# Row statistics of tile 2 computed once, and two other constants for instruction blocks in the planner, in a retention + SoLU + cosine-gate kernel

## The chip, the cores and the metric

One core of a Trainium2 chip. The time is that of one execution on the device in microseconds, from its start to its end; shown are medians over runs. The profile is one more execution, recorded by the hardware profiler; its own time stands beside its span, which runs from the first to the last recorded instruction.

## The reference

Three stages over 4 x 768 = 3072 tokens of width 512:

```python
# 1: retention, 4 batches x 8 heads, head width 64
state = gamma * state + k[t] (x) v[t]
y[t]  = scale * q[t] @ state
# 2: x is y with the heads side by side, (3072, 512)
h    = x @ w_in                       # 512 -> 1024
e    = exp(h - max(h)); sm = e / (sum(e) + 1e-9)
solu = h * sm
ln   = (solu - mean(solu)) / sqrt(var(solu) + 1e-6) * g_ln
x2   = ln @ w_out                     # 1024 -> 512
# 3
h2   = x2 @ w_in2                     # 512 -> 2048
out  = (h2 * cos(h2)) @ w_out2        # 2048 -> 512
```

max, sum, mean and var run over the 1024 columns of a row.

## The kernel before, in words

**Stage 1** goes in 24 steps of 128 tokens (2 pairs of batches x 12 chunks of 64 tokens). `load_step` (L366 on) brings a step's q, k and v in two transfers into one of four buffers `in` (in the listings `in_162` to `in_165`); `prep` scales keys and queries; `scores` and the step before multiply keys by queries into PSUM tile `sc` (L409), `masks` turns that into `s` on VectorE (L354); `step` computes the output `y` (L427) and the new state `S` (L415). What comes out of a step, split into a high and a low part `xh`, `xl`, is the left operand of stage 2: step n gives *tile* n, 128 tokens. Tiles 2 and 3 keep `xh`, `xl` in a corner of `o1h`, `o1l`.

**Stage 2** multiplies a tile by `w_in` (`mm1`, L633; four blocks k of the 512 inputs, two halves c of the 1024 columns, three products for each k: `w1h,xh`, `w1h,xl`, `w1l,xh`), into PSUM: `hA` (two banks of 512 columns), or, for tiles 0, 2 and 4, `hB` (three banks). Tile 0 has banks 0 and 1 of `hB`, tile 2 has banks 1 and 2: its half 0 shares bank 1 with tile 0's half 1. `norm(n)` then computes the row statistics of tile n from both halves: a maximum over 1024 columns (L651, VectorE), an Exp with its sum (ScalarE, L351, tile `u`), a product with its sum (L362, VectorE), a Square with its sum (ScalarE), a chain of one-column operations on tiles `sm` (`sm_77` to `sm_79`, three in turn), a power on POOL (L660) and the normalisation of `u` on VectorE (L664) or ScalarE. Then `transp` (L678) transposes four tiles at a time into PSUM tiles `tr`, which are opened where `hB` was once tile 4 is through (`open_tr`), and `mm2` (L703) multiplies by `w_out`.

`chunk(c, k, tiles)` issues the products of one k and one half c, the two with `w1h` first and `w1l` behind; `first(n, c)` issues all of one half, and calls `norm(n)` where c is 1:

```python
def first(n, c):
    for k in range(KD):
        mm1(n, c, k)
    if c == 1:
        norm(n)
```

Near the program's start tile 2's half 1 is issued before its half 0, as `first(2, 1)` (L1085), between the last products of tile 0 (`chunk(0, k, (0,))`, which calls `norm(0)`) and the scores of step 3. Half 0 follows later, as `first(2, 0)`, and then `norm(2)` by name. So `norm(2)` stands twice: once ahead of half 0, when bank 1 of `hB` still holds tile 0's columns, and once behind it. The second overwrites everything that the first has written.

**Stage 3** forms the products with `w_in2` and `w_out2` with seven half-size products in place of eight (L879, L960), the cosine between them on ScalarE and VectorE; weights are split on chip during stage 2, written to memory and read back.

**The order of the work** on each engine is the planner's. `Plan.add` records every operation with an engine, a cost and the keys that it reads and writes; `Plan.order` plays them through a model: TensorE takes one of the next 10 in program order (`WINDOW`), the other engines what can start first, among near equals what has the longest way to the end. The list that results is then issued as it stands, and the framework adds semaphores where tiles are shared; it sees `hB` as one tile. An engine posts its count only at instructions that another one waits for.

The model also counts TensorE's instructions (`ni`; a weight load and a matmul are two) in blocks of 256, the first ending after 256 - 63. When a block begins, the next one is taken to arrive `FETCH[1]` us later, or `FETCH[2]` if the time is past `FETCH[0]`; no operation of that block is placed sooner:

```python
fetched[0] += self.count[i]
if fetched[0] // self.BLOCK[1] > was:
    blocks.append(max(t + occ, blocks[-1]) + self.FETCH[1 if t < self.FETCH[0] else 2])
```

These are constants of the planner alone; they reach the chip only through the order.

Of the kernel before, what the change touches and what calls it, by code (L numbers as in the profile page):

```python
# [32 lines left out]
KD = DM // 128  # L33
# [15 lines left out]
class Plan:  # L49
# [17 lines left out]
    LOOK = .1  # L67
    FIRST = (16, 0.97, 0.6)
    BLOCK = (63, 256)
    FETCH = (30.0, 6.3, 4.0)  # L70

    def __init__(self):
        self.ops = []
# [49 lines left out]
    def order(self):  # L123
# [62 lines left out]
        while left:  # L186
# [36 lines left out]
            if e == "PE":  # L223
# [3 lines left out]
                if fetched[0] // self.BLOCK[1] > was:  # L227
                    blocks.append(max(t + occ, blocks[-1]) + self.FETCH[1 if t < self.FETCH[0] else 2])
            else:
# [28 lines left out]
def body(ctx: ExitStack, tc: tile.TileContext, qkv, consts,  # L258
# [126 lines left out]
    def prep(n):  # L385
        i = steps[n][1]
        if i:
            P.add("POOL", 1.2, lambda: nc.gpsimd.tensor_tensor(  # L388
                out=a_p[n % 2].rearrange("p (a b) t -> p a b t", b=2),
                in0=a_q[n % NA].rearrange("p (a b) t -> p a b t", b=2),  # L390
                in1=gat.unsqueeze(2).to_broadcast([128, NHP, 2, C]), op=ALU.mult),
                [("gat",), ("in", n % NA, 1)], [("x32", n % 2)], port=True)
        if has_state(n):
            k = a_kn[n % NA]
            for a in range(NHP):
                f = cs[:, 1, i, a:a + 1]
                act(k[:, a], k[:, a], AF.Copy, [("cs",), ("in", n % NA, 2)], [("ks", n % NA, a)], 0.295,
                    alt=("DVE", 0.2, lambda k=k[:, a], f=f: nc.vector.tensor_scalar(
                        out=k, in0=k, scalar1=f, scalar2=None, op0=ALU.mult), True), scale=f)
# [225 lines left out]
    def mm1(n, c, k, ms=(0, 1, 2)):  # L625
        h, hk = hbank(n, c)
        xh, xl = xhs[xb(n)], xls[xb(n)]
        xhk, xlk = xk[xb(n)]

        def mm():  # L630
            for m in ms:
                a, lo = ((xh, 0), (xl, 0), (xh, 1))[m]
                nc.tensor.matmul(out=h, lhsT=a[:, k], rhs=w1[lo][k][c], start=(k + m == 0), stop=(k == KD - 1 and m == 2))  # L633
        r = [xhk]
        if 0 in ms or 1 in ms:
            r += [("w1h", k, c)]
        if 1 in ms:
            r += [xlk]
        if 2 in ms:
            r += [("w1l", k, c)]  # L640
        P.add("PE", 0.2267 * len(ms), mm, r, [hk], lat=0.2267 * len(ms) + 0.25, ni=2 * len(ms))

    def norm(n):
        b = [hbank(n, c) for c in (0, 1)]
        h = h_of(n)
        hk = [b[0][1], b[1][1]]
        sm = sms[n % 3]
        smk = lambda *c: [("sm", n % 3, x) for x in c]
        u = us[n % UBUF]
        uk = [("u", n % UBUF, c) for c in (0, 1)]  # L650
        P.add("DVE", 1.135, lambda: nc.vector.tensor_reduce(  # L651
            out=sm[:, 0:1], in_=h, axis=AX.XY, op=ALU.max, negate=True), hk, smk(0))
        act(u, h, AF.Exp, hk + smk(0), uk + smk(1), 1.1, 1.35, bias=sm[:, 0:1], accum_out=sm[:, 1:2])
        stt(u, u, 1.0, h, ALU.mult, ALU.mult, hk, uk + smk(2), 1.18, accum_out=sm[:, 2:3])
        ts(sm[:, 3:4], sm[:, 2:3], -1.0 / FF1, None, ALU.mult, None, smk(2), smk(3), 0.07)
        act(junk, u, AF.Square, uk + smk(3), [("junk",)] + smk(4), 1.14, 1.38, bias=sm[:, 3:4], accum_out=sm[:, 4:5])
        ts(sm[:, 5:6], sm[:, 1:2], 1e-9, None, ALU.add, None, smk(1), smk(5), 0.07)
        stt(sm[:, 6:7], sm[:, 5:6], 1e-6, sm[:, 5:6], ALU.mult, ALU.mult, smk(5), smk(6), 0.07, port=True)
        stt(sm[:, 7:8], sm[:, 4:5], 1.0 / FF1, sm[:, 6:7], ALU.mult, ALU.add, smk(4, 6), smk(7), 0.07, port=True)
        P.add("POOL", 0.56, lambda: nc.gpsimd.tensor_tensor(out=sm[:, 8:9], in0=sm[:, 7:8], in1=mhalf, op=ALU.pow),  # L660
              smk(7), smk(8), port=True)
        tt(sm[:, 9:10], sm[:, 3:4], sm[:, 8:9], ALU.mult, smk(3, 8), smk(9), port=True, occ=0.07)
        act(u, u, AF.Identity, smk(8, 9), uk, 1.14,
            alt=("DVE", 0.75, lambda: nc.vector.tensor_scalar(  # L664
                out=u, in0=u, scalar1=sm[:, 8:9], scalar2=sm[:, 9:10], op0=ALU.mult, op1=ALU.add), True),
            scale=sm[:, 8:9], bias=sm[:, 9:10])
# [379 lines left out]
# [6 lines that stand above are left out]
    def chunk(c, k, tiles=(0, 1)):  # L1052
        for ms in ((0, 1), (2,)):
            for n in tiles:
                mm1(n, c, k, ms)
                if c == 0 and k == KD - 1 and 2 in ms:
                    norm(n)
# [24 lines left out]
    P.chained(False)  # L1082
    for k in range(KD):
        chunk(0, k, (0,))
    first(2, 1)  # L1085
    prep(3)
    scores(3)
    for k in range(KD):
# [171 lines left out]
```

## Time and profile before

| | |
|---|---|
| median of 3 runs | 839.0 us (837.82 to 840.07) |
| the profiled execution | 837.1 us, of which 835.3 us span |
| TensorE (PE) busy | 817.4 us, 98% |
| weight loads (PEld) | 717.0 us, 86% |
| VectorE (DVE) busy | 649.0 us, 78% |
| ScalarE (ACT) busy | 506.4 us, 61% |
| POOL busy | 48.6 us, 6% |
| mean granted TensorE clock | 0.999 |

TensorE is busy nearly throughout, so the time is its work and the gaps in it. In rows of the trace a matmul's length contains the part that overlaps the next one: full matmuls of 512 columns start 0.23 us apart, though each is 0.39 us long; VectorE's passes over 512 columns start 0.6 us apart, those over 1024 columns 1.14 us.

### The profile page before, as it was taken

The page shows a single profiled execution, that of the slowest core. Times are in us where ns is not written, and L with a number is a line of the kernel's source. Part 1 is how long each engine was busy: PE and PEld are TensorE (multiplying, and loading weights), DVE is VectorE, ACT ScalarE, POOL GpSimd, SP SyncE. Part 2 cuts the span into 40 slices and gives each one's busy share as a digit, 9 for nine tenths or more (in the row PEclk, how much of TensorE's full clock was granted, in tenths as well). Part 3 has the DMA queues.
Part 4 walks back from the last instruction along what each step waited for, and adds up shares of the span by engine and source line. Part 5 has one row for each costly group of instructions (what it writes and reads, how often), then busy time and mean ns, then how long its engine had stood idle before and what let it go on. Part 6 is the DMA issues. An engine that isn't in the chain of part 4 may idle for free.

```text
span 835.3 us, 18919 instructions
## 1 busy us (share of the span) xinstructions
PE 817.4 (98%) x7312; PEld 717.0 (86%) x7312; DVE 649.0 (78%) x1157; ACT 506.4 (61%) x893; POOL 48.6 (6%) x56
## 2 busy tenths in 40 slices
PE   5899999999999999999999999999999999999997
PEld 4778888888888888888889999888999988889997
DVE  4789988879888677338789993787999648779953
ACT  4688857656666466346785463676746446665452
POOL 2221210111101000000000000000000000000000
PEclk9999999999999999999999999999999999999999
DMA  9893699899976649246665688767667787666563
GB/s 353 326 336 114 194 320 342 270 322 300 323 271 224 219 161 319 86 131 195 192 207 184 198 257 246 233 192 197 201 195 209 198 271 194 196 191 188 181 193 83
DMA packets 93513, 188.19 MB, mean 225 GB/s; under 512 B 9712, under 2 KB 25328, under 8 KB 93424
## 3 DMA queue, kind: packets, MB, share of 16 engines
q1 hardware_dynamic: 92816, 186.41, 70.1%
q8 instruction: 58, 0.95, 0.5%
q10 hardware_dynamic: 608, 0.57, 0.2%
q14 instruction: 31, 0.25, 0.1%
HBM read 145.01 MB, written 41.94 MB: 224 GB/s over the span
## 4 chain that ended last, share of the span: by engine, by line
PE 90%; DMA 4%; DVE 3%; SPq 1%; ACT 1%; issue 1%; ACTq 0%
PE U L879 27%; PE pa L960 15%; PE hA L633 13%; PE y L703 11%; PE U L960 8%; PE pb L960 4%; PE y L427 4%; PE hB L633 2%; PE tr L678 2%; PE tr L703 2%; DMA big<-w_in_dram 1%; DMA in<-qkv_dram 1%; PE sc L409 1%; DVE u L362 1%; DMA y1d<-ys 1%
## 5 line engine op out<-in xcount | busy, mean ns | idle before, releaser
L960 PE MATMUL pa<-wr,gh 128*128 128x256 f32 x768 | 139.8, 283 | 0.0
L902 ACT ACTIVATE gh<-A 128x512 fp32r<-128x512 f32 x144 | 90.7, 630 | 78.6 <-PE pa L960 43.6
L904 DVE TENSOR_TENSOR gl<-A,gh 128x512 fp32r<-128x512 f32 x144 | 98.6, 686 | 29.7 <-ACT gh L902 29.6
L960 PEld LDWEIGHTS pa<-wr,gh 128*128 128x128 f32 x768 | 120.2, 192 | 0.5
L960 PE MATMUL pa<-wr,gl 128*128 128x256 f32 x384 | 108.7, 283 | 0.0
L703 PE MATMUL y<-lt,o1h 128*128 128x512 f32 x304 | 101.9, 399 | 0.0
L960 PEld LDWEIGHTS pa<-wr,gl 128*128 128x128 f32 x384 | 73.7, 192 | 0.0
L960 PE MATMUL U<-wr,gh 128*128 128x256 f32 x384 | 70.3, 283 | 0.0
L703 PEld LDWEIGHTS y<-lt,o1h 128*128 128x128 f32 x304 | 57.1, 188 | 12.2
L633 PE MATMUL hA<-w1h,xh 128*128 128x512 f32 x160 | 64.4, 403 | 0.3 <-DVE u L362 0.2
L633 PE MATMUL hA<-w1l,xh 128*128 128x512 f32 x160 | 62.5, 391 | 0.0
L633 PE MATMUL hA<-w1h,xl 128*128 128x512 f32 x160 | 62.4, 390 | 0.0
L960 PEld LDWEIGHTS U<-wr,gh 128*128 128x128 f32 x384 | 59.9, 192 | 0.0
L703 PE MATMUL y<-lt,o1l 128*128 128x512 f32 x152 | 59.3, 390 | 0.0
L351 ACT ACTIVATE st<-wt 128x512 fp32r<-128x512 f32 (+1 forms) x60 | 35.8, 601 | 33.7 <-DMA wd<-st 17.8
L960 PE MATMUL U<-wr,gl 128*128 128x256 f32 x192 | 54.3, 283 | 0.0
L354 DVE TENSOR_TENSOR st<-wt,st 128x512 fp32r<-128x512 f32 (+1 forms) x60 | 40.5, 678 | 17.0 <-ACT st L351 16.8
L427 PE MATMUL y<-s,in 64*64 64x64 f32 x736 | 45.0, 226 | 1.1 <-DVE s L354 1.1
L427 PEld LDWEIGHTS y<-s,in 64*64 64x64 f32 x736 | 36.4, 138 | 9.2 <-issue 4.6
L427 PE MATMUL y<-x,st 64*64 64x64 f32 x672 | 40.3, 218 | 0.0
L388 POOL TENSOR_TENSOR x<-in,c_all 128x512 f32<-128x512 f32 x22 | 30.5, 1385 | 141.2 <-issue 88.2
L960 PEld LDWEIGHTS U<-wr,gl 128*128 128x128 f32 x192 | 36.9, 192 | 0.0
(180 smaller groups left out, 2082.6 us busy)
## 6 DMA issues: line engine op xcount, KB each, us to landing
wr<-wd SPq DMA_DIRECT2D x168, 256.0 KB, 3.0
wr<-td SPq DMA_DIRECT2D x168, 256.0 KB, 3.0
in<-qkv_dram SPq DMA_DIRECT2D x48, 512.0 KB, 6.2
wd<-st SPq DMA_DIRECT2D x28, 512.0 KB, 4.9
td<-st SPq DMA_DIRECT2D x24, 512.0 KB, 3.5
raw<-w_in_dram SPq DMA_DIRECT2D x16, 511.8 KB, 6.0
raw<-w_out_dram SPq DMA_DIRECT2D x16, 511.8 KB, 5.0
y1d<-ys SPq DMA_DIRECT2D x24, 256.0 KB, 3.7
```

The costliest lines, as they stand in the source:

```text
L351: return P.add("ACT", occ, lambda: nc.scalar.activation(out=out, in_=in_, func=func, **kw), r, w, lat, alt=alt)
L354: return P.add("DVE", occ, lambda: nc.vector.tensor_tensor(out=out, in0=a, in1=b, op=op), r, w, port=port)
L362: return P.add("DVE", occ, lambda: nc.vector.scalar_tensor_tensor(out=out, in0=a, scalar=s, in1=b, op0=op0, op1=op1, **kw), r, w, port=port)
L388: P.add("POOL", 1.2, lambda: nc.gpsimd.tensor_tensor(out=a_p[n % 2].rearrange("p (a b) t -> p a b t", b=2), in0=a_q[n % NA].rearrange("p ( ...
L427: nc.tensor.matmul(out=ybank(n)[0][o, j], lhsT=a[r, j], rhs=b[r, j], start=not part, stop=bool(part) or not later)
L633: nc.tensor.matmul(out=h, lhsT=a[:, k], rhs=w1[lo][k][c], start=(k + m == 0), stop=(k == KD - 1 and m == 2))
L678: nc.tensor.transpose(out=trs[s][:, t * 128:(t + 1) * 128], in_=us[(4 * g + t) % UBUF].rearrange("p c f -> p (c f)")[:, j * 128:(j + 1) * ...
L703: nc.tensor.matmul(out=y1(), lhsT=w[:, j, ds], rhs=lts[j][:, a], start=(j + m == 0), stop=(j == K1 - 1 and m == 2))
L879: nc.tensor.matmul(out=U(), lhsT=p2["wr"][w][:, kk, lo], rhs=p2["x"][m][xl][:, kk], start=(kk + q == 0 and m in (0, 1, 4)), stop=(kk == 1 ...
L902: P.add("ACT", 0.54, lambda: nc.scalar.activation(out=p2["gh"][i], in_=src(), func=AF.Copy), [key], [("gh", i)], after=(*p2["cos_hook"], * ...
L904: P.add("DVE", 0.6, lambda: nc.vector.tensor_tensor(out=p2["gl"][i], in0=src(), in1=p2["gh"][i].bitcast(F32), op=ALU.subtract), [key, ("gh ...
L960: nc.tensor.matmul(out=o, lhsT=p2[x][g][:, t * 128:t * 128 + 128], rhs=v[:, lo], start=(fresh and t % 2 == 0 and i == 0), stop=(s == 7 and ...
```

## The change

Tile 2's half 1 is issued with `chunk(1, k, (2,))` for each k: the same products, without the call of `norm(2)` that stood ahead of half 0. `norm(2)` now stands once, behind half 0. And `FETCH` holds three other numbers: the next block arrives 5.8 us after a block's begin up to 60 us, 4.5 us later on (before: 6.3 us up to 30 us, then 4.0).

```diff
@@ -67,7 +67,7 @@
     LOOK = .1
     FIRST = (16, 0.97, 0.6)
     BLOCK = (63, 256)
-    FETCH = (30.0, 6.3, 4.0)
+    FETCH = (60.0, 5.8, 4.5)
 
     def __init__(self):
         self.ops = []
@@ -1082,7 +1082,8 @@
     P.chained(False)
     for k in range(KD):
         chunk(0, k, (0,))
-    first(2, 1)
+    for k in range(KD):
+        chunk(1, k, (2,))
     prep(3)
     scores(3)
     for k in range(KD):
```

The planner makes another list of it. TensorE's differs in four places: two around the end of tile 2's half 1, one at the first transposes, and one group of four transposes near the end of stage 2. VectorE's, ScalarE's and the transfers' lists are the same up to about 31 us and then differ until the end of stage 2. TensorE, from the last products of tile 0's half 0 (`hB<-..,xh_126`) to tile 1's first (`hA`); `..,o1h` and `..,o1l` are tile 2's half 1, `sc<-in_165` the scores of step 3; the semaphores that an instruction waits for stand in brackets. Before:

```order
L633 MATMUL hB<-w1h_89,xh_126 128x512 [waits Activation_49]
L633 MATMUL hB<-w1h_89,xl_128 128x512
L409 MATMUL sc<-in_165 64x64 [waits DMAHW0_49]
L409 MATMUL sc<-in_165 64x64 x7
L633 MATMUL hB<-w1l_97,xh_126 128x512 [waits DVE_49]
```

and, ten matmuls on, the end of the same stretch as a piece of the difference:

```order
 L633 MATMUL hB<-w1h_90,o1h 128x512
 L633 MATMUL hB<-w1h_90,o1l 128x512
+L633 MATMUL hB<-w1l_99,xh_126 128x512 [waits DVE_49]
 L633 MATMUL hB<-w1l_98,o1h 128x512
-L633 MATMUL hB<-w1l_99,xh_126 128x512 [waits DVE_49]
 L633 MATMUL hB<-w1h_92,o1h 128x512
 L633 MATMUL hB<-w1h_92,o1l 128x512
-L633 MATMUL hB<-w1l_100,o1h 128x512
-L409 MATMUL sc<-in_165 64x64 x8
+L633 MATMUL hB<-w1l_100,o1h 128x512 [waits DVE_49]
+L409 MATMUL sc<-in_165 64x64 [waits DMAHW0_49]
+L409 MATMUL sc<-in_165 64x64 x15
```

The eight scores that stood ahead of `w1l_97` have moved behind tile 2's half 1, to the other eight; tile 0's last product (`w1l_99,xh_126`) stands one place earlier; and the last product of tile 2's half 1 (`w1l_100,o1h`) has got a wait for VectorE.

VectorE at the same place, from the last of the weights' low halves to tile 0's product (`u_104`). Before:

```order
L354 TENSOR_TENSOR w1l_99<-big_123,w1h_91 128x512 [waits Activation_49]
L398 TENSOR_SCALAR in_162<-in_162,c_all 128x128 [waits DMAHW3_49]
L398 TENSOR_SCALAR in_162<-in_162,c_all 128x128
L651 TENSOR_REDUCE sm_77<-hB 128x1 [waits PE_49]
L651 TENSOR_REDUCE sm_79<-hB 128x1
L354 TENSOR_TENSOR s_167<-sc,c_all 128x256 [waits PE_49]
L362 SCALAR_TENSOR_TENSOR u_104,sm_77<-u_104,hB 128x1024 [waits Activation_49]
L362 SCALAR_TENSOR_TENSOR u_106,sm_79<-u_106,hB 128x1024
```

Now:

```order
L354 TENSOR_TENSOR w1l_99<-big_123,w1h_91 128x512 [waits Activation_49]
L398 TENSOR_SCALAR in_162<-in_162,c_all 128x128 [waits DMAHW3_49]
L398 TENSOR_SCALAR in_162<-in_162,c_all 128x128
L651 TENSOR_REDUCE sm_77<-hB 128x1 [waits PE_49]
L398 TENSOR_SCALAR in_163<-in_163,c_all 128x128 [waits DMAHW5_49]
L398 TENSOR_SCALAR in_163<-in_163,c_all 128x128
L354 TENSOR_TENSOR s_167<-sc,c_all 128x256 [waits PE_49]
L354 TENSOR_TENSOR s_167<-sc,c_all 128x256
L398 TENSOR_SCALAR in_163<-in_163,c_all 128x128
L362 SCALAR_TENSOR_TENSOR u_104,sm_77<-u_104,hB 128x1024 [waits Activation_49]
```

Tile 2's early maximum (`sm_79<-hB`) and product (`u_106`) are gone, scalings of keys stand there, and both mask passes `s_167` follow the maximum of tile 0. In the built program the count for which `w1l_100,o1h` waits is the one that this maximum posts, and the maximum's own wait is for a count that TensorE posts at `w1h_92,o1l`, the matmul just ahead of `w1l_100,o1h`.

VectorE some 25 us later, from just behind the maximum of tile 3 (`sm_77<-hA`) and two passes `o1l<-big_116`, `o1l<-big_117`, to the maximum of tile 4 (`sm_78<-hB`); `big` and `o1l` are weights of `w_out` on their way to two halves. Now:

```order
L362 SCALAR_TENSOR_TENSOR big_118<-big_118,top_158 128x512
L362 SCALAR_TENSOR_TENSOR u_107,sm_77<-u_107,hA 128x1024
L358 TENSOR_SCALAR sm_77<-sm_77 128x1 x2
L362 SCALAR_TENSOR_TENSOR sm_77<-sm_77 128x1
L362 SCALAR_TENSOR_TENSOR o1l<-big_118,gcol,o1h 128x512
L362 SCALAR_TENSOR_TENSOR big_119<-big_119,top_159 128x512
L362 SCALAR_TENSOR_TENSOR big_120<-big_120,top_158 128x512
L362 SCALAR_TENSOR_TENSOR sm_77<-sm_77 128x1
L398 TENSOR_SCALAR in_163<-in_163,c_all 128x128
L362 SCALAR_TENSOR_TENSOR o1l<-big_119,gcol,o1h 128x512
L651 TENSOR_REDUCE sm_78<-hB 128x1
```

Between the same two maxima the list before has one pass each of `big` and `o1l`, the normalisation of tile 0 and the product of tile 3; now it has three of `big`, four of `o1l` and the product, and behind the second maximum stand one small operation, a state pass, a mask pass and the product of tile 4 (`u_108<-u_108,hB`) in place of two small ones, the state pass, the normalisation of tile 2, another small one, the mask pass and that product. On TensorE the first eight transposes (`tr`), whose first waits for VectorE, stand behind 12 products of tile 5, and behind 15 before.

## Rows read from the trace of the kernel before

**Rows 1.** The page, busy time (share of the span) and instructions of each engine.

```profile
PE 817.4 (98%) x7312; PEld 717.0 (86%) x7312; DVE 649.0 (78%) x1157; ACT 506.4 (61%) x893; POOL 48.6 (6%) x56
```

**Rows 2.** By stretches, core 0: us, busy us (x instructions) of each engine, clock, DMA share, GB/s.

```profile
40.00:50.00 10.00, 8.44 (x155) 6.87 (x155) 9.61 (x26) 7.54 (x14) 3.25 (x4) 1.00 0.89 330
50.00:60.00 10.00, 8.21 (x156) 6.81 (x155) 7.84 (x17) 7.88 (x19) 3.21 (x3) 1.00 0.96 338
...
sum 835.30, PE 817.45 PEld 717.02 DVE 649.05 ACT 506.38 POOL 48.63; mean PE 35.54 PEld 31.17 DVE 28.22 ACT 22.02 POOL 2.11
```

**Rows 3.** Waits of TensorE, whole span: total us, times, longest us.

```profile
PE sc L409 <- DMA in<-qkv_dram: 5.7, 1, 5.7
PE hA L633 <- issue: 1.8, 1, 1.8
```

**Rows 4.** Timeline of TensorE, 29 to 35 us: start us, length us, instruction.

```profile
29.71 0.68 PE L409 MATMUL sc<-in 64*64 64x64 f32 x16
30.38 0.50 PE L633 MATMUL hB<-w1l,xh 128*128 128x512 f32 x1
...
33.71 0.39 PE L633 MATMUL hB<-w1h,o1l 128*128 128x512 f32 x1
33.94 0.39 PE L633 MATMUL hB<-w1l,o1h 128*128 128x512 f32 x1
34.25 0.68 PE L409 MATMUL sc<-in 64*64 64x64 f32 x16
34.87 0.50 PE L633 MATMUL hA<-w1h,xh 128*128 128x512 f32 x1
```

**Rows 5.** Timeline of VectorE, 29 to 50 us.

```profile
29.65 0.68 DVE L354 TENSOR_TENSOR w1l<-big,w1h 128x512 fp32r<-128x512 f32 x1
...
34.36 2.35 DVE L651 TENSOR_REDUCE sm<-hB 128x1 f32<-128x1024 f32 x2 [2.11 <-PE hB L633]
...
40.29 1.21 DVE L362 SCALAR_TENSOR_TENSOR u<-u,hB 128x1024 f32<-128x1024 f32 x1
...
49.76 0.81 DVE L664 TENSOR_SCALAR u<-u,sm 128x1024 f32<-128x1024 f32 x1
```

**Rows 6.** Timeline of TensorE, 39.6 to 41.9 us, in brackets idle time and its releaser.

```profile
39.68 0.22 PE L409 MATMUL sc<-in 64*64 64x64 f32 x2
41.56 0.50 PE L633 MATMUL hB<-w1h,o1h 128*128 128x512 f32 x1 [1.66 <-DVE u L362]
```

**Rows 7.** The page, DMA queue of instructions: packets, MB, share of 16 engines.

```profile
q8 instruction: 58, 0.95, 0.5%
```

**Rows 8.** The same queue from 41.9 to 42.1 us, and from 53.2 to 53.3 us.

```profile
q8 instruction: 1, 0.02, 27.5%
...
q8 instruction: 1, 0.02, 58.2%
```

**Rows 9.** By stretches of 128 matmuls each; those across an edge are counted on both sides.

```profile
38.30:44.76 6.46, 4.80 (x140) 3.89 (x133) 5.62 (x9) 4.92 (x12) 1.27 (x1) 1.00 0.97 379
...
50.28:55.60 5.32, 3.57 (x134) 3.08 (x135) 4.08 (x8) 5.06 (x14) 2.00 (x2) 1.00 0.96 326
```

**Rows 10.** Timeline of TensorE, 53.3 to 55.9 us.

```profile
55.64 0.39 PE L633 MATMUL hA<-w1h,o1h 128*128 128x512 f32 x1 [1.79 <-issue]
```

**Rows 11.** Timeline of VectorE, 56 to 68 us.

```profile
56.52 1.23 DVE L651 TENSOR_REDUCE sm<-hA 128x1 f32<-128x1024 f32 x1 [1.74 <-PE hA L633]
...
58.78 0.69 DVE L362 SCALAR_TENSOR_TENSOR big<-big,top 128x512 int32<-128x512 int32 x1
...
60.92 0.75 DVE L362 SCALAR_TENSOR_TENSOR o1l<-big,gcol,o1h 128x512 fp32r<-128x512 f32 x1
...
61.96 1.22 DVE L651 TENSOR_REDUCE sm<-hB 128x1 f32<-128x1024 f32 x1 [0.29 <-PE hB L633]
...
66.33 1.21 DVE L362 SCALAR_TENSOR_TENSOR u<-u,hB 128x1024 f32<-128x1024 f32 x1
```

**Rows 12.** Timeline of TensorE, 67 to 68.5 us.

```profile
67.69 1.06 PE L678 MATMUL tr<-ident,u 128*128 128x128 f32 x8
```

## The prediction

> **What bounds the kernel now.** I began with the page's busy times [rows 1]: TensorE works 817.4 of 835.3 us, so only 17.9 us of gaps can be won or lost unless matmuls are added or taken away, and this change does neither. The stretches show where gaps lie [rows 2]: the clock is at full speed (1.00), and 40 to 50 and 50 to 60 us lack 1.56 and 1.79 us of TensorE. The waits of TensorE [rows 3] name two of the long ones: 5.7 us ahead of the first matmul, for the first transfer, which the change does not touch, and 1.8 us before a product into `hA`, put down to "issue", that is to no semaphore. The timelines show the rest: 1.66 us before the product at 41.56, released by VectorE [rows 6], and the 1.79 us of "issue" end at 55.64 [rows 10]. Everything that the change moves lies between 29 us and the end of stage 2, so I go through these gaps in order of time, and ask of each whether it goes, stays, or comes back elsewhere.
>
> **Term 1, the early statistics leave: -1.7 us.** VectorE loses an early maximum (two maxima take 2.35 us together, so some 1.2), a product at 40.29 of 1.21 us and a normalisation at 49.76 of 0.81 us [rows 5]: 3.2 us of work, and ScalarE loses an Exp and a Square beside it. Nearly all lies beside matmuls and is worth nothing by itself. One piece is on TensorE's path. The product at 40.29 reads bank 1 of `hB`, which tile 2's half 0 is about to overwrite; it ends at 41.50, and the first matmul of that half starts at 41.56 [rows 5, 6]. Without it only tile 0's own product has to be done there. That needs tile 0's maximum, one Exp and itself, in a row some 1.2 us each [rows 5], behind a maximum that now starts near 34 us; it is done near 38, while TensorE is busy until 39.9. So the whole gap of 1.66 us goes.
>
> **Term 2, a new wait at the end of tile 2's half 1: +1.5 us.** In the lists of the change the last product of that half, `w1l_100,o1h`, waits for the count that tile 0's maximum posts, and that maximum itself waits for the matmul just ahead. So a maximum of 1024 columns, 1.22 us long when it stands alone [rows 11], now lies between two neighbours on TensorE. Before, the neighbours started 0.23 us apart (33.71 and 33.94) [rows 4], and the maximum started at 34.36, 0.03 us after the last one's end (33.94 + 0.39 = 34.33) [rows 4, 5]. Now: the predecessor's whole 0.39, the maximum's 1.22, some 0.1 for the two signals (an estimate: one is 0.03 as above, the other 0.06, from the product's end at 41.50 to the start at 41.56 [rows 5, 6]), less 0.23, makes 1.47. Queued behind it on TensorE are 16 scores and all of tile 1. Nothing hides it.
>
> **Term 3, eight scores no longer fill a wait: +0.5 us.** `w1l_97` is written by VectorE from 29.65 to 30.33 and read by the matmul at 30.38 [rows 4, 5]. Before, TensorE spent the wait on eight scores (29.71, 0.68 us; the trace counts each row of the list double). Now it stands idle there for about 0.75 us (30.38 - 29.71, and the change of shape that is saved), and the eight cost their time later, 0.62 (34.25 to 34.87) [rows 4], less some 0.1 for one change of shape fewer (ahead of a score block matmuls start 0.31 apart, 33.94 to 34.25, in place of 0.23 [rows 4]).
>
> **Term 4, TensorE runs into its own instructions earlier: +1.3 us.** The queue of instructions moved 58 packets of 16 KB [rows 7], and TensorE issues 14,624 of the program's instructions [rows 1], so a packet is a block of some 252, or about 126 matmuls. When the matmul at 55.64 waits for "issue" [rows 10], a packet of that queue is in flight from 53.2 us [rows 8]: TensorE goes on 2.4 us after its start. That block's predecessor began at 50.28, so the block came 5.36 us after it. The packet at 41.9 us [rows 8], plus the same 2.4, gives 44.3, which is 6.0 us after its predecessor's begin at 38.30; it was wanted at 44.76, so there were 0.4 us to spare [rows 9]. Exactly there term 1 takes 1.7 us out of TensorE's time: the stretch of 6.46 becomes 4.8, and the block, if it still takes 6.0 to 6.1, comes 1.3 late. The upper bound is 1.7 (it took at most 6.46, since no wait showed). The lower one is nothing, if it comes within 4.8; with the 5.36 of the other block it would be 0.6. I take 1.3 because that is this very block, at nearly the same time of the same transfers (DMA share 0.97 [rows 9]). The 1.79 us at 55.64 stay: the order of TensorE's instructions between is the same, and so is what each block holds.
>
> Beside these rows stands a rule. The Trainium skill (Runtime: NRT & Kernel Launch, Instruction fetch mechanics) says that the sequencer fetches the next 16 KiB, 256 instructions, while it executes the current ones, so that crossing such a border is mostly hidden. By that rule term 4 is nothing and the sum below 1.1. The trace here agrees on the size of a block and disagrees on the hiding, with 1.79 us of idle "issue" while a packet is in flight.
>
> **Term 5, the first transposes wait for VectorE: +0.8 us.** They go where `hB` was, so they wait for tile 4's product. Measured from the start of tile 3's maximum (56.52), TensorE reached them 11.17 us later, at 67.69 [rows 11, 12], when that product (66.33, 1.21 us) had just ended, at 67.54. Now they stand three matmuls, 0.7 us, earlier: 10.5. VectorE has more to do between the two maxima: four passes `o1l` and three `big` at their pace of 0.6 to 0.66 us (single rows 0.75 and 0.69 [rows 11]), two passes over 1024 columns at 1.15 and some 0.5 of small operations make 7.3 in place of 61.96 - 56.52 = 5.44. From the second maximum to the product's end it has less: 1.15, two passes of 0.6 and 1.15, 3.5 to 4 in all, in place of 5.6 (61.96 to 67.54). Together 10.9 to 11.4, so a wait of 0.4 to 0.9 and some signalling: I take 0.8. Bounds: nothing, if the passes keep their closest pace, and 2.4, if the second stretch stays at 5.6, for then the product ends at 7.3 + 5.6 = 12.9.
>
> **At no cost.** The other constants make no instruction; they act only through the list. One POOL operation is gone; no gap that I take rests on POOL. The transfers that change places on SP's queue and the scalings of keys now ahead of tile 0's mask passes concern steps read later or halves that are there by then; I allow -0.5 to +1 for them and for the changed list after 70 us.
>
> **The sum:** -1.7 + 1.5 + 0.5 + 1.3 + 0.8 = +2.4 us on a profiled execution of 837.1 us, so 839.5. That execution is 1.9 below the median of 839.0, so against medians I forecast **841.4 us**.
>
> **The rivals.** *Instructions come in time:* term 4 is nothing, the sum +1.1, the time 840.1. For it speaks that a block came in 5.36 us at another place, against it the stall with a packet in flight. *Slower, because the transposes wait:* tile 4's product stays as late behind its maximum as it was, the wait is 2.4 in place of 0.8, the sum +4.0, the time 843.0. It decides as soon as the wait passes 0.9 us, since then the change is slower by more than 0.3% (2.5 us, about what a measurement of this kernel can tell). For it speaks that VectorE's list there also holds waits for ScalarE that were not filled before; against it that a normalisation stands there no longer. *The gain is kept:* the new wait of term 2 does not bite (the count is posted in time by something else) and instructions come in time: -1.7 + 0.5 + 0.8 = -0.4, 838.6. For it speaks only that I read that wait off a list and not off a trace. That the early statistics do not leave is excluded by VectorE's list.
>
> **How the numbers follow.** The forecast has 0.45, its own range 840.0 to 842.8; instructions in time 0.25; the waiting transposes 0.20; the kept gain 0.10. Range: 838.0 to 844.0, from just below the kept gain to the waiting transposes with term 4 at its bound. Faster than 836.5 needs the kept gain and another 2 us that no row shows: 0.05. Slower than 841.5 are the waiting transposes (0.20), just under half of the forecast (0.20) and a little of the second case: 0.42. The rest, 0.53, is no change.
>
> **What would show it.** The gap at 41.56 gone; one of about 1.5 us at 34 us before the last product of tile 2's half 1, and one of 0.75 before `w1l_97`; an "issue" gap near 45 us, and the old one of 1.8 us near 57; a wait for VectorE before the first `tr`. Wrong, if TensorE's idle time between 29 and 70 us falls by more than 1 us, or if the difference arises after 70 us.

## The result: 845.6 us, slower by 0.84%

Four runs of the change have a median of 845.62 us (845.01 to 847.16), beside 838.62 for the kernel before, timed with them; the ratio is 1.0084, with a 95% interval of 1.0065 to 1.0104. The forecast was 841.4, in a range of 838.0 to 844.0: the sign is right, the size is not, and the time lies outside the range. The profiled execution took 847.2 us, of which 845.4 are span; that of the kernel before took 837.1, so the two profiles lie 10 us apart where the medians lie 7.0 apart. The page's busy times, beside [rows 1]:

```profile
PE 822.1 (97%) x7312; PEld 718.5 (85%) x7312; DVE 647.6 (77%) x1165; ACT 500.3 (59%) x872; POOL 52.4 (6%) x55
```

VectorE and ScalarE are busy for less time, as the change promises, but VectorE by 1.4 us only, where term 1 takes 3.2 us from it. In e3_drop below, which takes out the early statistics and moves nothing, the page reads

```profile
PE 818.0 (98%) x7312; PEld 716.7 (86%) x7312; DVE 646.8 (77%) x1148; ACT 504.0 (60%) x889; POOL 49.6 (6%) x55
```

Against it the change has 17 instructions more on VectorE and 17 fewer on ScalarE: passes `in<-in,c_all`, scalings of keys, which the new list gives to VectorE. TensorE, with the same 7312 matmuls, has 4.7 us more of busy time, and 845.4 - 822.1 = 23.3 us of idle time in place of 17.9. Its waits over the whole span, beside [rows 3]:

```profile
PE hA L633 <- issue: 2.8, 1, 2.8
PE tr L678 <- DVE lt L690: 2.6, 3, 1.3
...
PE hB L633 <- DVE sm L651: 1.3, 1, 1.3
...
PE hA L633 <- DVE u L362: 0.9, 2, 0.7
PE S L415 <- issue: 0.8, 2, 0.5
PE tr L678 <- ACT ys L708: 0.5, 1, 0.5
```

The wait for the early product ([rows 6]) is gone; all of these are new or longer than before. In order of time, the timeline of TensorE (start, length, instruction, idle time ahead of it and its releaser):

```profile
31.27 0.50 PE L633 MATMUL hB<-w1l,xh 128*128 128x512 f32 x1 [0.61 <-DVE w1l L354]
...
34.58 0.39 PE L633 MATMUL hB<-w1h,o1l 128*128 128x512 f32 x1
36.28 0.50 PE L633 MATMUL hB<-w1l,o1h 128*128 128x512 f32 x1 [1.32 <-DVE sm L651]
36.71 1.15 PE L409 MATMUL sc<-in 64*64 64x64 f32 x32
...
46.75 0.27 PE L415 MATMUL S<-in 64*64 64x64 f32 x2 [0.47 <-issue]
...
52.80 0.27 PE L415 MATMUL S<-in 64*64 64x64 f32 x1 [0.28 <-issue]
...
59.28 0.50 PE L633 MATMUL hA<-w1h,o1h 128*128 128x512 f32 x1 [2.82 <-issue]
...
60.93 0.63 PE L633 MATMUL hB<-w1h,xh 128*128 128x512 f32 x1
61.35 0.63 PE L633 MATMUL hB<-w1h,xl 128*128 128x512 f32 x1
...
138.13 1.25 PE L678 MATMUL tr<-ident,u 128*128 128x128 f32 x8 [0.90 <-DVE lt L690]
...
148.73 0.50 PE L633 MATMUL hA<-w1h,xh 128*128 128x512 f32 x1 [0.73 <-DVE u L362]
...
340.92 0.66 PE L678 MATMUL tr<-ident,u 128*128 128x128 f32 x4 [0.47 <-ACT ys L708]
...
347.22 0.66 PE L678 MATMUL tr<-ident,u 128*128 128x128 f32 x4 [1.30 <-DVE lt L690]
```

At 36.28 stands the wait of term 2; three waits for instructions follow up to 60 us where one was; at 60.93 matmuls start 0.42 us apart in place of 0.23, so the clock has fallen; behind 130 us come waits at transposes, of which the kernel before has one, of 0.3 us, and one ahead of a product into `hA`. By stretches (us, busy us of each engine, clock, DMA share, GB/s):

```profile
60.50:64.00 3.50, 3.50 (x10) 2.69 (x10) 3.50 (x5) 1.74 (x3) 0.00 (x0) 0.51 0.72 290
...
64.00:66.00 2.00, 2.00 (x10) 1.65 (x9) 2.00 (x7) 2.00 (x4) 0.00 (x0) 1.00 0.02 8
```

The granted clock is 0.51, the lower of the two levels, for 3.5 us. To see where the time goes I set each matmul's start against that of its counterpart (by its place in TensorE's order) in the profile of before. The change is later by 0.9 us at 29 us, 1.2 at 41, 3.8 at 56, 5.4 at 60, 5.1 at 70, 4.9 at 130, 7.8 at 250 and 10.0 at 340 and to the end. The 0.9 at 29 us is scatter: up to there the two lists are the same, and profiles of the experiments with that same beginning stand at -1.1 to +1.3. What is left has two halves: some 4 us up to 70 us, of which 1.6 came with the fallen clock, and some 5 behind 130 us, where I had allowed -0.5 to +1.

### The profile page after: what moved, and what is told of

Read it like the earlier page. It is cut to its first block, busy times and chain, and to the rows that moved or that the text cites. A ratio compares the mean times of both kernels' runs of the same rounds, so it can differ in the third digit from the quotient of the medians.

```text
span 845.4 us, 18897 instructions
## 1 busy us (share of the span) xinstructions
PE 822.1 (97%) x7312; PEld 718.5 (85%) x7312; DVE 647.6 (77%) x1165; ACT 500.3 (59%) x872; POOL 52.4 (6%) x55
## 4 chain that ended last, share of the span: by engine, by line
PE 66%; DMA 2%; DVE 1%; ACT 1%; issue 0%; ACTq 0%; DVEq 0%
PE U L879 27%; PE pa L960 16%; PE U L960 8%; PE pb L960 4%; PE y L703 4%; PE hA L633 3%; PE tr L703 2%; DMA raw<-y1d 2%; PE tr L678 1%; PE y L427 1%; DVE lt L690 0%; DVE raw L354 0%; DMA out_dram<-oo 0%; ACT lt L688 0%; DVE x6l L767 0%
## 5 line engine op out<-in xcount | busy, mean ns | idle before, releaser
L354 DVE TENSOR_TENSOR st<-wt,st 128x512 fp32r<-128x512 f32 (+1 forms) x60 | 38.8, 654 | 18.7 <-ACT st L351 18.6
L690 DVE TENSOR_TENSOR lt<-tr,lt 128x512 fp32r<-128x512 f32 x48 | 31.5, 685 | 8.1 <-ACT lt L688 8.1
```

The lines of the kernel that those rows point to most:

```text
L354: return P.add("DVE", occ, lambda: nc.vector.tensor_tensor(out=out, in0=a, in1=b, op=op), r, w, port=port)
L690: P.add("DVE", 0.6, lambda: nc.vector.tensor_tensor(out=lts[j][:, 1], in0=trs[s], in1=lts[j][:, 0].bitcast(F32), op=ALU.subtract), [("hb", ...
```

## The experiments

Eleven kernels, each timed in five rounds against the kernel before on the same chip; its medians there were 839.65 us (the first four), 838.98 (the next four) and 839.83 (the last three). The first four and the last three ran on one chip, the four between on another, so a run is compared by its difference from the kernel before of its own set. Those medians lie 1.9 to 2.7 us above the one profiled execution of the kernel before (837.1 us), so differences of two profiles come out larger than differences of medians. Most experiments take a list of the planner and cut, splice or rearrange it. For that `P.plan(once, fetch)` gives the planner's list with the early statistics once or twice and with the old or new constants (`OLD`, `NEW`), as triples of an operation's number, its function and its time in the plan; `issue` picks what is issued. `only_of` marks operations that stand in one version alone, `moved(l, ids, ahead)` puts some operations ahead of another one. The pieces of code show the lines that matter, not the whole edit.

### The two parts alone

```diff
-    FETCH = (30.0, 6.3, 4.0)
+    FETCH = (60.0, 5.8, 4.5)
```

> The two constants alone, the early statistics stay. Theory (the loss comes from what the planner's new list does: a product held by tile 0's maximum at about 36 us, late evacuations of transposes after 130 us): the list is new here too, and its last product of tile 2's half 1 waits for a VectorE count as it does in the change, while the wait for the early product near 41 us stays; so slower than before by 2 to 6 us, 841 to 845. Rival (the constants do nothing, the removal of the statistics shifts TensorE into its instruction blocks): within 1 us of before.

Measured: 840.71 us, ratio 1.0010 (0.9997 to 1.0023). The trace has the held product (1.3 us) and the gap near 41 us, as the theory said, but the loss of 2 to 6 us that I expected is not there: +1.1 us is about the rival's 1 us. The rival's reason, that the constants do nothing, fails too, since the list is a new one.

```diff
-    FETCH = (60.0, 5.8, 4.5)
+    FETCH = (30.0, 6.3, 4.0)
```

(The edit is against the change, so the early statistics go and the constants stay as before.)

> The early statistics go, the constants stay as before, and the planner makes its own list. Its list is that of the change up to about 44 us, with the same product held by the maximum. Theory (about 3.3 us of the profile's 10 are lost up to 50 us with the held product, the idle wait ahead of w1l_97 and the first block, and 4 after 130 us by the list there): the first part as in the change, the late part by luck of the list; 841 to 847. Rival (the constants are to blame): 837 to 839.5.

Measured: 839.80 us, ratio 1.0001 (0.9987 to 1.0015). Again a miss. The held product, the wait ahead of `w1l_97` and the first wait for instructions (0.43 us) are as in the change, but in place of the stall ahead of 59.28 stands one of 1.24 us at 53.5, and behind 70 us only 1.6 us are lost. So neither part loses by itself what both lose together. Each of the four combinations has another list, and what follows from a list was to be looked for.

### The list of before without the early statistics

```diff
+def issue(P):
+    return [fn for i, fn, _ in P.plan(False, OLD) if P.only_of(i) != "stat"]
```

> The list of before, word for word, with only the early statistics of tile 2 taken out: the work goes, nothing moves. Theory (the list is to blame, not the removal): the gap of 1.66 us at 41.56 goes, no product of tile 2's half 1 waits for a maximum, the instruction block wanted near 43 us gives back 0.6 to 1.3 us, the clock stays at full speed; against before -1.7 to 0, 837 to 838.6. Rival (an earlier TensorE runs into its instruction blocks, stands long enough for the clock to fall, whatever the list): slower than before by 2 us or more, a granted clock near 0.8 between 60 and 70 us.

Measured: 838.54 us, ratio 0.9990 (0.9976 to 1.0003). It is the cleanest trial of what the removal is worth. Against the profile of before TensorE is 1.7 us earlier at 44 us: term 1, to the tenth. At 46 us it is 0.4 us later:

```profile
45.27 0.27 PE L440 MATMUL S<-in 64*64 64x64 f32 x1 [1.90 <-issue]
...
55.58 0.39 PE L658 MATMUL hA<-w1h,o1h 128*128 128x512 f32 x1 [1.19 <-issue]
```

(In most of the experiments' kernels the lines stand 25 to 37 further down.) The packet of instructions started at 42.9 us, and TensorE went on 2.4 us later, as it did in [rows 8, 10]. What the removal gives at 41 us the next instruction block takes back at 45: 2.1 us, more than the 0.6 to 1.3 that I expected.

### The change's list up to 70 us, that of before behind

```diff
+def issue(P):
+    a, b = P.plan(True, NEW), P.plan(False, OLD)
+    cut = next(n for n, (_, _, t) in enumerate(a) if t >= 70.0)
+    done = {i for i, _, _ in a[:cut]}
+    return [fn for _, fn, _ in a[:cut]] + [fn for i, fn, _ in b if i not in done and not P.only_of(i)]
```

> The change's list up to 70 us of the plan's time, the list of before behind it. Theory (some 4 us of the loss arise after 130 us, at transposes whose evacuations the new list places late): 3 to 4.5 us faster than the change, 841 to 843, with no wait of a transpose for lt or ys over 0.5 us after 100 us, and the losses up to 70 us unchanged (held product 1.3, stall near 59 us of 2.8 with the clock's fall behind it). Rival (those waits follow from the early delay and not from the list): 845 to 846.

Measured: 841.65 us, ratio 1.0027 (1.0012 to 1.0041): +2.0 us, where the change has +7.0. So by medians the first 70 us cost about 2 us and the list behind them the rest, and no transpose waits over 0.4 us for `lt` behind 100 us: the theory holds. In its profile TensorE is 3.6 us late at 70 us and 4.3 at the end, against the one profile of before. The losses up to 70 us are not quite those of the change, though I had expected them unchanged: the long wait for instructions is 2.25 us, the clock did not fall, and the wait of term 5 shows:

```profile
PE hA L661 <- issue: 2.3, 1, 2.3
...
PE tr L706 <- DVE u L390: 1.3, 1, 1.3
```

### Why instruction blocks come late: the loads of w_out

In the change, step 7's load of q, k and v waits on SP's queue until all scores of step 3 are through; the loads of `w_out` behind it wait with it. The transfers' queue (start, length, transfer) of the change:

```profile
28.97 0.42 SPq L506 DMA_DIRECT2D big<-w_out_dram  x1
37.94 0.33 SPq L375 DMA_DIRECT2D in<-qkv_dram  x1
38.31 1.50 SPq L506 DMA_DIRECT2D big<-w_out_dram  x3
```

and of e3_drop, where those scores stand where they stood before:

```profile
28.11 0.42 SPq L531 DMA_DIRECT2D big<-w_out_dram  x1
35.03 0.33 SPq L400 DMA_DIRECT2D in<-qkv_dram  x1
35.40 1.61 SPq L531 DMA_DIRECT2D big<-w_out_dram  x3
```

The loads of `w_out` thus come when instruction packets are wanted. In e3_drop the transfers' engines had room for some of them: from 34 to 36 us their share of busy time is 0.07. (Not more: the expectation below has them nearly idle from 28.5 to 35 us, but from 28 to 35 the share is 0.76.) So seven loads of `w_out` were put ahead of that load, first in e3_drop:

```diff
+def issue(P):
+    l = [x for x in P.plan(False, OLD) if P.only_of(x[0]) != "stat"]
+    l = moved(l, (187, 192, 197, 202, 207, 281, 286), 634)
+    return [fn for _, fn, _ in l]
```

> e3_drop with one thing moved: the seven loads of w_out (big1 to big7) stand on SP's queue ahead of step 7's load of q, k and v, behind which they wait from 28.5 to 35 us while the transfers' engines stand nearly idle. Theory (a block of TensorE's instructions comes late because its packet queues behind data that fills the 16 engines): with less data in flight between 40 and 56 us its packets start sooner, the stalls of 1.9 us at 45.3 and of 1.2 at 55.6 shrink or go, so 1.5 to 3 us faster than e3_drop: 835.5 to 837. Rival (a packet's start depends on TensorE's own progress, not on the data): the stalls stay within 0.3 us, 838 to 839.

Measured: 834.17 us, ratio 0.9943 (0.9925 to 0.9961), faster than both kernels. Its transfers, and its only wait for instructions up to 63 us:

```profile
28.00 6.22 SPq L540 DMA_DIRECT2D big<-w_out_dram  x8
35.12 16.69 SPq L409 DMA_DIRECT2D in<-qkv_dram  x7
```

```profile
43.57 0.27 PE L449 MATMUL S<-in 64*64 64x64 f32 x1 [0.31 <-issue]
```

Packets start at 41.3, 45.4 and 49.6 us here, in e3_drop at 42.9, 46.4 and 53.3. TensorE's order is the same in both, and up to 43 us so are its times, to 0.1 us. So where seven loads stand on SP's queue bears on when a packet starts, and the rival is excluded. That a packet queues behind data that fills the engines is not shown: they are about as full around the first packet in e3_drop (first row) as in e5_loads (second row; the last three numbers are clock, DMA share and GB/s).

```profile
40.00:46.00 6.00, 4.10 (x82) 3.20 (x86) 3.09 (x6) 3.56 (x6) 1.30 (x1) 1.00 1.02 402
...
40.00:46.00 6.00, 5.69 (x143) 4.62 (x143) 4.48 (x8) 4.09 (x8) 1.78 (x2) 1.00 0.96 385
```

Only from 50 to 56 us is the share much lower, 0.63 in place of 0.96. The same move in the change's own list:

```diff
+def issue(P):
+    l = P.plan(True, NEW)
+    l = moved(l, (187, 192, 197, 202, 207, 281, 286), 634)
+    return [fn for _, fn, _ in l]
```

> The change's own list with the same seven loads moved ahead of step 7's. Theory (the stalls at 46.7, 52.8 and above all the 2.8 us ahead of 59.3 come from blocks queued behind data, and the clock's fall behind the last follows from standing still): the stall near 59 is under 1.5 us, the clock stays at 1.00 up to 70 us, 3 to 5 us less up to 65 us; the waits behind 130 us stay: 841 to 843. Rival (the stalls are not due to the data): 845 to 846.

Measured: 842.63 us, ratio 1.0044 (1.0027 to 1.0061): +3.7 us, where the change has +7.0. The stalls are shorter, but one of 1.76 us is left, so that the bound of 1.5 was missed, and the clock falls behind it all the same, which the theory excluded. Up to 65 us TensorE loses 3.3 us in this profile and 4.5 in the change's, each counted from 29 us on: 1.2 less, not the 3 to 5 expected.

```profile
56.27 0.50 PE L667 MATMUL hA<-w1h,o1h 128*128 128x512 f32 x1 [1.76 <-issue]
```

```profile
58.00:60.00 2.00, 2.00 (x6) 1.52 (x6) 2.00 (x3) 1.18 (x2) 0.00 (x0) 0.50 0.92 346
```

And in the kernel before, early statistics kept:

```diff
+def issue(P):
+    l = P.plan(False, OLD)
+    l = moved(l, (187, 192, 197, 202, 207, 281, 286), 634)
+    return [fn for _, fn, _ in l]
```

> The kernel before with its early statistics, and the seven loads of w_out moved ahead of step 7's as in e5_loads. Theory (the removal is worth the gap of 1.66 us as soon as no instruction block is late): the stall at 55.6 shrinks as in e5_loads, the gap ahead of 41.56 stays, so 1.4 to 2 us slower than e5_loads: 835.6 to 836.3. Rival (the loads' place is all, the removal nothing): within 0.5 us of e5_loads, 834.2.

Measured: 836.17 us, ratio 0.9957 (0.9942 to 0.9972): -3.7 us, where e5_loads has -4.8. The gap for the early product is in its place:

```profile
42.55 0.50 PE L667 MATMUL hB<-w1h,o1h 128*128 128x512 f32 x1 [1.66 <-DVE u L396]
```

The two medians lie 2.0 us apart, as expected, but they are of two chips; against the kernel before on each it is 1.2, which is neither the theory's 1.4 to 2 nor the rival's 0.5, and the intervals (1.3 us and 1.5 us to either side) are as wide. The profiles, counted from 29 us on, say the same: e5_loads is 1.7 us ahead at 44 us and 1.2 at 56, since it alone has the wait of 0.31 us. So the removal keeps most of what its gap is long, once instruction blocks come nearly in time.

### The held product

Tile 0's maximum (operation 117) goes behind the last product of tile 2's half 1, in the list of e4_tail; each engine's own order stays, only that product's wait goes:

```diff
+    l = moved(l, (117,), 156)
```

> e4_tail with tile 0's maximum moved behind the last product of tile 2's half 1 in the list, nothing else. Theory (that product waits 1.3 us for the maximum alone, but the instruction blocks behind are bound to the transfers): the gap of 1.3 us near 36 us is gone, and 0.5 to 1.3 us of it come back as longer stalls for instructions near 46 and 58 us; against e4_tail 0 to 0.8 us faster, 840.8 to 841.7. Rival (the time gained is kept): 840.3.

Measured: 841.42 us, ratio 1.0021 (1.0005 to 1.0037), which cannot be told from e4_tail's 1.0027. The gap at 36 us is gone, and the waits for instructions grow from 0.45, 0.28 and 2.25 us in e4_tail to

```profile
45.68 0.27 PE L452 MATMUL S<-in 64*64 64x64 f32 x2 [1.01 <-issue]
...
58.20 0.80 PE L670 MATMUL hA<-w1h,o1h 128*128 128x512 f32 x1 [3.35 <-issue]
```

That is 1.4 us more, so they take back all of the 1.3. And the clock fell in this profile, which it did not in e4_tail's:

```profile
60.00:62.00 2.00, 2.00 (x6) 1.54 (x5) 2.00 (x3) 0.86 (x1) 0.00 (x0) 0.50 0.83 334
```

Of the 12 runs 11 have a mean granted clock of 0.998 or less, beside 8 of 12 in e4_tail. So term 2 is real, and taking it away gained nothing that could be measured: the blocks behind came later, and lower clock adds to that.

### Behind 70 us

The list of before up to 300 us, the change's behind it:

(against e4_tail)

```diff
-    a, b = P.plan(True, NEW), P.plan(False, OLD)
-    cut = next(n for n, (_, _, t) in enumerate(a) if t >= 70.0)
+    a, b = P.plan(False, OLD), P.plan(True, NEW)
+    cut = next(n for n, (_, _, t) in enumerate(a) if t >= 300.0)
```

> The list of before up to 300 us of the plan's time, the change's behind it, so only the last transposes of stage 2 differ. Theory (of the 4 us behind 70 us, some 2 arise at the transposes between 330 and 350 us, where the change's list evacuates ys and lt late): 1.7 to 2.3 us slower than before, with waits of a transpose for ys (0.5) and for lt (1.3) there. Rival (these waits need the delay of what stands ahead): within 0.5 us of before.

Measured: 843.01 us, ratio 1.0047 (1.0031 to 1.0063): +4.0 us, twice what I expected. The trace shows why:

```profile
315.93 0.73 PE L732 MATMUL y<-lt,o1h 128*128 128x512 f32 x2 [1.77 <-DVE lt L719]
...
336.29 0.66 PE L707 MATMUL tr<-ident,u 128*128 128x128 f32 x4 [0.98 <-ACT ys L737]
```

The first is at the join of the lists, and neither list has it alone; without it, some 2.2 us are left to the last transposes, as in the change. The other way round, the change's list up to 300 us and that of before behind (against e4_tail):

```diff
-    cut = next(n for n, (_, _, t) in enumerate(a) if t >= 70.0)
+    cut = next(n for n, (_, _, t) in enumerate(a) if t >= 300.0)
```

> The change's list up to 300 us of the plan's time, the list of before behind it. Theory (the losses behind 70 us fall into two independent parts, 2.9 between 130 and 250 us and 2.2 at the last transposes): as the change up to 300 us, without the waits at 340 and 347; against the change -2.2, 843.4, if the join of the lists costs nothing; the join in e8_end cost one wait of 1.8 us, so up to 845. Rival (the late waits follow from the delay ahead of them): 845.5 or more, with a wait of a transpose over 1 us near 347.

Measured: 845.11 us, ratio 1.0063 (1.0039 to 1.0086), +5.3 us, just above the 845 that I had allowed for a join that costs. With e4_tail at +2.0 that leaves 3.3 to the list between 70 and 300 us, and some 1.7 of the change's 7.0 to what is behind. The intervals are 1.2 us (e4_tail) and 2.0 us (e11_mid) to either side, so the halves are rough; and a wait of 1.0 us at the transposes of 341 us stayed with the old list, so the two parts aren't independent:

```profile
341.03 0.66 PE L707 MATMUL tr<-ident,u 128*128 128x128 f32 x4 [1.00 <-DVE lt L719]
```

One wait by itself. Ahead of the transposes at 347.22 VectorE has, in the change, passes on `raw` that wait for a transfer, and the evacuation `lt` behind them:

```profile
345.15 0.69 DVE L354 TENSOR_TENSOR raw<-raw,raw 128x512 f32<-128x512 f32 x1 [2.21 <-DMA raw<-y1d]
...
346.49 0.68 DVE L690 TENSOR_TENSOR lt<-tr,lt 128x512 fp32r<-128x512 f32 x1
```

Three such passes go behind two evacuations; no other engine's order changes:

```diff
+    l = P.plan(True, NEW)
+    l = moved(l, (2023, 2032, 2026), 1600)
```

> The change's own list with one move on VectorE: three passes on raw, which wait for a transfer of y1d until 345 us, go behind the two evacuations lt that stand behind them. Theory (the wait of 1.3 us of the transposes at 347.2 is that order alone, and nothing behind takes it back): the wait is gone, TensorE is 1.0 to 1.3 us less behind the kernel before at 350 us than in the change's profile (2.2 lost between 325 and 350 us there, 0.9 to 1.2 here), median about 844.4. Rival (the passes on raw are needed in time for the products with w_in2): the 1.3 us come back at a product U before 400 us.

Measured: 845.50 us, ratio 1.0069 (1.0045 to 1.0092): +5.7 us against the kernel before of its set, where the change has +7.0; the intervals overlap, so this says little. In the profile the wait is gone, and between 325 and 350 us TensorE loses 1.5 us in place of 2.2, not the 0.9 to 1.2 expected, since the wait for `ys` ahead of it is 0.81 us in place of 0.47 and one of 0.30 follows:

```profile
343.12 0.65 PE L712 MATMUL tr<-ident,u 128*128 128x128 f32 x4 [0.81 <-ACT ys L742]
...
350.67 0.66 PE L712 MATMUL tr<-ident,u 128*128 128x128 f32 x4 [0.30 <-DVE lt L724]
```

So that wait came from the order on VectorE. That it explains its share of the median is not shown.

## Why the prediction was wrong, step by step

**Term 1 (-1.7) was right.** It is -1.7 at 44 us in e3_drop, and again between e10_loads_before and e5_loads.

**Terms 2 and 3 (+1.5, +0.5) were right.** From 34.58 to 36.28 are 1.70 us, less 0.23 is 1.47. In e4_tail, whose profile has no scatter at 29 us, TensorE is 0.4 us late at 41 us; -1.7 + 1.5 + 0.5 = +0.3 was forecast. Only term 2's price was not shown to be a loss of its own: e7_max got nothing measurable back by taking it away.

**Term 4 (+1.3) was the right wait with the wrong size.** I counted one late block and let the stall at 55.6 stay. Three blocks come late: in e4_tail the waits cost 1.9 us more than before (0.4 at 44 us, 2.3 at 60), in the change 2.6 (1.2 to 3.8). In e3_drop, where the late block is the only thing behind term 1, it takes 2.1, above my upper bound of 1.7, and the later stall shrinks to 1.19. The sentence that failed is "if it still takes 6.0 to 6.1": from 38.30 to 45.27 are 7.0 us. A packet does not come at a fixed time after the block ahead begins, and why it came a microsecond later than before in e3_drop stays open: up to 41 us TensorE and the transfers of SP's queue start at the same times, to 0.1 us, but for the gap that is gone. What e5_loads shows is that the place of seven loads moves the first packet by 1.6 us and the next two by 1.0 and 3.7, while TensorE itself runs ahead by then. "At no cost" asked of the transfers only who reads them. In the change the loads behind step 7's load move from 35.4 to 38.3 us; what that shift costs was not tried by itself, and e1_fetch, where they stand at 32.5 us, has waits of 0.44 and 2.20 us all the same. By the rule of the Trainium skill (Runtime: NRT & Kernel Launch, Instruction fetch mechanics) that crossing from one block to the next is mostly hidden, none of these waits would show. Behind 70 us the profiles agree with it, for no wait put down to "issue" there is longer than 0.2 us; ahead of that the change differs, with 2.82 us, and e5_loads agrees, with 0.31.

**Term 5 (+0.8) was of the right kind.** In e4_tail and e11_mid, with the same list there, the first transposes wait 1.3 us for tile 4's product. In the change's profile they don't wait: TensorE, slowed by the fallen clock, comes later than that product. Nor do they in the other profiles of this list in which the clock fell (e6_loads_change, e7_max, e9_lt).

**A term was missing: the clock.** It cost 1.6 us at 60 us in the profile of the change (3.8 us late at 56 us, 5.4 at 60, measured against the kernel before, whose clock is 1.00 there [rows 2]). No row of before showed it, though the stall that precedes it is there with 1.79 us [rows 10].

**The step that failed most is "I allow -0.5 to +1 for them and for the changed list after 70 us".** The list behind 70 us cost about 5 us, of +7.0, and the prediction's own sign of being wrong, "if the difference arises after 70 us", came true for most of it. The bound stands there without a reason: I had read TensorE's order behind 70 us, found four transposes moved, and left the other engines out. But VectorE's and ScalarE's lists are new up to the end of stage 2, and the transposes go through two PSUM tiles, so a late evacuation can stop TensorE, as the 1.30 us at 347.22 show. [Rows 1] held a warning: VectorE is 78% busy, so an evacuation can be placed behind passes of 0.6 to 1.2 us. And of the 17 key scalings that VectorE has more than in e3_drop, ten lie between 130 and 250 us, where TensorE loses 2.9 us; e2_once has two more there and TensorE loses 0.6. That they are the cause was not tried.

The rival *transposes wait* named one such place and gave 843.0, but in the change's profile that wait is not there, so that it lies nearest is luck; *instructions come in time* and *the gain is kept* did not happen in the change. What stays open is why the lists of both parts alone are near zero (1.0010, 1.0001) and that of both together is not: the runs show in which stretch each list loses, not a rule by which the planner came to it. Part of the "near zero" is the clock. The kernel before has a mean granted clock of 0.998 or less in 18 of its 35 runs of that set, e1_fetch in 1 of 12, e2_once in none. Among runs at 0.999 or more alone the means are 838.6, 840.5 and 839.8, so there each part loses, 1.9 and 1.2 us. The waits between 130 and 250 us were not tried one by one.

## What to carry to other kernels

When a planner writes the order, a changed operation or constant changes every list behind it: cost the new list on every engine to its end, or keep the old list and take the operation out of it (e3_drop), so that the part under trial is alone. A gap that is closed is worth something only if what bounds the next stretch is not already waiting; here it was TensorE's own instruction blocks, and moving seven loads ahead of one blocked load on the same queue made them come sooner: it was worth 0.57% together with the removal, and 0.43% without it. For each transfer that moves, ask what else moves through the transfers' engines at its new time, not only who reads it. And compare runs with their own set, and at a like clock: a difference of 2 us between two medians can be the chip's or the clock's.

## What the runs showed that I had not expected

The clock fell, for 3.5 us of the change's profile, 1.3 us after a stall of 2.82 us had ended. Such a stall doesn't decide it: before, one of 1.79 us was followed by no fall, in e6_loads_change one of 1.76 was; in e11_mid one of 2.81 was not. The mean granted clock of an execution tells of such falls, though roughly, for it also counts the end (0.50 from 833 us on in the profile of before): in the first set the kernel before averaged 838.0 us in the 6 runs with a mean of 1.000, and 840.7 in the 18 with 0.998 or less. All four runs of the change have 0.998 or less. So part of the 7.0 us may be more frequent falls, and the forecast's basis, one profile without one, could not show their price. But they are not the bulk of it: e11_mid, with the change's list up to 300 us, has 0.999 or more in five of six runs, and these average 844.8 us, 6.1 above such runs of the kernel before in its set.
